# P transposes and row sums behind the eighth K tile, a last weight load in two single-row pieces, and a result signalled per column tile

## The chip, the cores and the metric

The kernel runs on one core of one Trainium2 chip. Times are device microseconds (us) of one execution. The kernel before takes 193.18 us, the median of four runs (193.08 to 195.44).

## What is computed

One decode step (one token, batch 8, width 512) of a block made of sliding-window attention over a cache, then a small multi-layer perceptron. Inputs are bfloat16. Cut to what matters:

```python
# attention: 32 query heads, 8 key/value heads, head size 128, window of the last 2048 of 8192 positions
q = layernorm(x) @ wq
scores = einsum("bhqd,bhkd->bhqk", q, k_window) * 128 ** -0.5
h = x + einsum("bhqk,bhkd->bhqd", softmax(scores), v_window) @ wo
# MLP: for one token the token-shift branch is zero, so x1 = xb
xb = layernorm(h)
out = h + xb + gelu(layernorm(xb) @ w3) @ w4      # w3: 512 x 1792, w4: 1792 x 512
```

For each of the 8 batches the windows of K and of V are 4 MB each. With `wq`, `wo`, `w3` and `w4` the core reads 79 MB from HBM.

## The kernel before, in words

**Loads.** SyncE (SP) issues nearly all loads on one queue, in a fixed list: `wq`, then K of batch 0 (two halves of four KV heads, 2 MB each), the first V half of the last batch, a first part of `wo`; then, for b = 0 to 6, the two K halves of batch b+1 and the two V halves of batch b; then the other V half of the last batch, the rest of `wo`, `w3`, `w4`. Every half has one buffer ("slot"), so SP waits before it reloads it: for a K half until TensorE has read the previous contents (`sem_Thi`, L239 to L240), for a V half until the PV product has read them (`sem_PV`, L241 to L242). `w4` (L260 to L267) goes into slot 0 once the last batch's first K half has been read, in pieces of 8, 4 and 2 blocks of 128 rows; within a piece, four (or, in the last, two) consecutive rows of `w4` lie together in a partition, and `w3_col` picks the matching columns of `w3`.

**A block.** TensorE works through 8 blocks, block i for batch i (`pe_block`, L561). The steps are:

- T(t), t = 0 to 7 (`pe_T`): 16 transposes of a K tile into one of two PSUM buffers `kT_ps`. ScalarE copies the low half out (`act_Elo`), VectorE the high half (`dve_Ehi`). A T that reuses a buffer waits for both copies of the tile two before.
- QK(t) (`pe_QK`): 4 matmuls of the copied tile with the queries, which collect the scores of all eight tiles in one bank of `S_ps`.
- `dve_max` (row maximum, five instructions), then `act_exp` twice (the exponentials into `P_sb`, the row sums into `lsum`).
- P(0), P(1) (`pe_P`): 8 transposes each of the previous batch's `P_sb`, into the same two `kT_ps` buffers; `dve_pT` masks them into `pT_sb`.
- LB (`pe_LB`): the row sums of the previous batch; `dve_rL` takes their reciprocal.
- PV (`pe_PV`): 128 matmuls of the previous batch's `pT_sb` with V; `dve_O1` scales, `pe_OP` reorders, `act_OP` stores into `opl`.

All orders are written by hand: TensorE's in `pe_block`, ScalarE's and VectorE's in the lists `AC` and `DV` (L602 to L619). In the kernel before, TensorE's block is: T0 to T3; P0, P1, LB of the previous batch; QK0, QK1; T4, QK2, T5, QK3, T6, QK4, T7, QK5; QK6, QK7; PV and OP of the previous batch. VectorE does `dve_pT` twice and `dve_rL` between its fourth and fifth copy. T4 and T5 take over the buffers of P0 and P1 and so wait for `dve_pT`.

**The end.** `pe_last` does P, LB, PV and OP of the last batch; then come the `wo` projection, the two layer norms, `w3`, gelu, and `pe_fin`: 14 blocks of `w4`, four matmuls each, one for each quarter of the 512 columns ("column tile" j, at partitions 32j). `pe_fin` waits for each piece of `w4` and signals after its last matmul. VectorE (`dve_final`) copies quarters 0 and 1, ScalarE (`act_final`) quarters 2 and 3, and SP stores the result.

Of the kernel before, what the change touches and what calls it, by code (L numbers as in the profile page):

```python
# [21 lines left out]
FC = F // 128  # L22
# [6 lines left out]
NT = 4  # L29
# [7 lines left out]
def bass_sequential_preLN__sliding_block_cached__mixer_s_mlp__decode_kernel(  # L37
# [24 lines left out]
    with es:  # L62
        sb = lambda shape, dtype, name: es.enter_context(nc.sbuf_tensor(name, shape, dtype))
        ps_t = lambda shape, dtype, name: es.enter_context(nc.psum_tensor(name, shape, dtype))
        S = lambda name: es.enter_context(nc.semaphore(name))
# [61 lines left out]
        NQ = 4  # L127
# [15 lines left out]
        sem_x = S("sem_x")  # L143
        sem_wq = S("sem_wq")
        sem_w3 = [S(f"sem_w3_{i}") for i in range(2)]
        sem_w4 = [S(f"sem_w4_{i}") for i in range(3)]
        sem_wo = [S(f"sem_wo{i}") for i in range(3)]
        sem_out = S("sem_out")

# [67 lines left out]

        NJ = DH // 4
        WO_CUT = [0, 8, 24, 32]
        W4_CUT = [0, 8, 12, 14]  # L220

        order = [("k", 0), ("k", 1), ("vl", 0), ("wo", 0)]
        for b in range(NB - 1):
# [191 lines left out]
        def need(e, sem, n):  # L415
            d = n - taken.setdefault(sem, 0)
            if d > 0:
                taken[sem] = n
                log.append((sem, d))
                if e is not None:  # L420
                    e.wait_ge(sem, d).then_inc(sem, -d)  # L421

        def pe_T(e, i, t):
            p = 2 * NT * i + t
            gq = t // NT
            if t % NT == 0:
                need(e, sem_k[gq], 16 * (i + 1))
            if t in (4, 5):
                need(e, sem_pT, 2 * i + t - 3)
            elif t in (2, 3, 6, 7):  # L430
                need(e, sem_Elo, p - 1)
                need(e, sem_Ehi, p - 1)
            if e is None:
                return
            k0 = t % NT * CT * DH
            src = slots[:, gq, k0:k0 + CT * DH]
            for c in range(CT):
                ins = e.matmul(kT_ps[t % 2][:, c * 128:(c + 1) * 128], src[:, c * 128:(c + 1) * 128],  # L438
                               perm_b[:, :], is_transpose=True)
                if c == CT // 2 - 1:  # L440
                    ins.then_inc(sem_Tlo, 1)
                if c == CT - 1:
                    ins.then_inc(sem_Thi, 1)

        def pe_P(e, i, half):
            need(e, sem_exp, 2 * i + half + 1)
            n = min(2 * NT * i + 3 + half, 2 * NT * NB)
            need(e, sem_Elo, n)
            need(e, sem_Ehi, n)
            if e is None:  # L450
                return
            for c in range(CT // 2):
                k = half * CT // 2 + c
                ins = e.matmul(kT_ps[half][:, c * 128:(c + 1) * 128], P_sb[:, k * 128:(k + 1) * 128],  # L454
                               perm_p[:, :], is_transpose=True)
            ins.then_inc(sem_PT, 1)
# [9 lines left out]
        def pe_QK(e, i):  # L466
            b, t = divmod(i, 2 * NT)
            gq, qi = divmod(t, NT)
            need(e, sem_Elo, i + 1)
            need(e, sem_Ehi, i + 1)  # L470
            if t == 0:
                need(e, sem_qc, b + 1)
            if e is None:
                return
            kv = kT_sb[:, i % NKT, :].rearrange("d (c g p) -> d g c p", p=PP, g=GL)
            o = 32 - R - R * t
            for gl in range(GL):
                ins = e.matmul(S_ps[32 * gl:32 * (gl + 1), 0, :], qcur[:, GL * gq + gl, o:o + 32],  # L478
                               kv[:, gl, :, :], start=(t == 0), stop=(t == 2 * NT - 1),
                               tile_position=(0, 32 * gl), skip_group_check=True)  # L480
            ins.then_inc(sem_QK, 1)
# [25 lines left out]
        def pe_LB(e):  # L507
            if e is not None:
                for half in range(2):
                    ins = e.matmul(LB, lspread[:, :, :].rearrange("p q h -> p (q h)"), lsum[:, half:half + 1],  # L510
                                   start=(half == 0), stop=(half == 1))
                ins.then_inc(sem_LB, 1)
# [6 lines left out]
        def dve_pT(e, b, half):  # L519
            e.wait_ge(sem_PT, 2 * b + half + 3)  # L520
            if b < 0 and half == 0:
                e.wait_ge(sem_pool, POOL_PT)
            m = mask16[:, :, :]
            h0 = half * CT // 2
            e.tensor_tensor(bass.AP(tensor=pT_sb[:, :, :, :].tensor, offset=h0 * NT * 48,  # L525
                                    ap=[[CT * NT * 48, 128], [48, CT // 2 * NT], [32, 2], [1, 16]]),
                            kT_ps[half][:, 0:W // 2].rearrange("p (c a x) -> p c a x", a=2, x=16),
                            bass.AP(tensor=m.tensor, offset=m.offset, ap=[m.ap[0], [0, CT // 2 * NT], [0, 2], [1, 16]]),
                            ALU.mult).then_inc(sem_pT, 1)
# [30 lines left out]

        def pe_block(e, i, later=None):  # L561
            p = 2 * NT * i
            for t in range(NT):
                pe_T(e, i, t)
            pe_P(e, i, 0)
            pe_P(e, i, 1)
            pe_LB(e)
            pe_QK(e, p)
            pe_QK(e, p + 1)
            for t in range(NT, 2 * NT):  # L570
                pe_T(e, i, t)
                pe_QK(e, p + t - 2)
            pe_QK(e, p + 6)
            pe_QK(e, p + 7)
            if i == 0:
                return
            with nullcontext() if e is None else e.If_ne(later, 0):
                log.append("later")
                for gq in range(2):
                    need(e, sem_v[gq], 16 * i)  # L580
                    if e is not None:
                        pe_PV(e, 2 + gq, gq)
                pe_OP(e, i - 1)
# [18 lines left out]
        for i in range(NB):  # L602
            p = 2 * NT * i
            for t in range(2 * NT):
                AC.append(lambda e, n=p + t: act_Elo(e, n))
                DV.append(lambda e, n=p + t: dve_Ehi(e, n))
                if t == 3:
                    DV.append(lambda e, i=i: dve_pT(e, i - 1, 0))
                    DV.append(lambda e, i=i: dve_pT(e, i - 1, 1))
                    if i:  # L610
                        DV.append(lambda e, i=i: dve_rL(e, i - 1))
            AC.append(lambda e, i=i: act_exp(e, i, 0))
            AC.append(lambda e, i=i: act_exp(e, i, 1))
            DV.append(lambda e, i=i: dve_max(e, i))
            if i + 1 < NB:
                DV.append(lambda e, i=i: dve_qc(e, i + 1))
            if i:
                DV.append(lambda e, i=i: dve_O1(e, i - 1))
                AC.append(lambda e, i=i: act_OP(e, i - 1))  # L619
# [99 lines left out]
        PEP_H3 = ev_pe.next()  # L719

        def w3_col(kc, fc):
            j = 4 if fc < W4_CUT[2] else W4_CUT[3] - W4_CUT[2]
            c0 = fc // 4 * 4
            return w3_sb[:, kc, c0 * 128:(c0 + j) * 128].rearrange("r (p j) -> r j p", j=j)[:, fc - c0, :]

        def pe_h3(e):
# [17 lines left out]
            e.activation(gT[:, :], misc[:, H3], ACT.Gelu_apprx_tanh).then_inc(sem_actP, 1)  # L744
        AC.append(act_gelu)

        PEP_FIN = ev_pe.next()

        def pe_fin(e):
            e.wait_ge(sem_dveP, DVEP_RES)  # L750
            for half in (hpx_hi, hpx_lo):
                for k in range(KC):
                    e.matmul(fin_ps[32 * k:32 * k + B, :], half[:, k * B:(k + 1) * B], ident_b[:, :],
                             start=(half is hpx_hi), stop=False, tile_position=(0, 32 * k), skip_group_check=True)
            e.wait_ge(sem_actP, ACTP_G)
            ins = None
            for fc in range(FC):
                if fc in W4_CUT:
                    e.wait_ge(sem_w4[W4_CUT.index(fc)], 16)
                for j in range(NQ):  # L760
                    ins = e.matmul(fin_ps[32 * j:32 * j + B, :], gT[:, fc * B:(fc + 1) * B],  # L761
                                   w4_sb[:, fc, j * DQ:(j + 1) * DQ], start=False, stop=(fc == FC - 1),
                                   tile_position=(0, 32 * j), skip_group_check=True)
            ins.then_inc(sem_peP, 1)
        PE.append(pe_fin)

        DVEP_OUT_READY = ev_dve.next()

        def dve_final(e):
            e.wait_ge(sem_peP, PEP_FIN)  # L770
            for j in range(NQ // 2):
                ins = e.tensor_copy(out_sb[:, j * DQ:(j + 1) * DQ], fin_ps[32 * j:32 * j + B, :])  # L772
            ins.then_inc(sem_dveP, 1)
        DV.append(dve_final)
# [1 line left out]
        ACTP_OUT_READY = ev_act.next()  # L776

        def act_final(e):
            e.wait_ge(sem_peP, PEP_FIN)
            for j in range(NQ // 2, NQ):  # L780
                ins = e.activation(out_sb[:, j * DQ:(j + 1) * DQ], fin_ps[32 * j:32 * j + B, :], ACT.Copy)
            ins.then_inc(sem_actP, 1)
        AC.append(act_final)
# [47 lines left out]
```

## Time and profile before

| quantity | value |
|---|---|
| median of four runs | 193.18 us (193.08 to 195.44) |
| the profiled execution, own time | 194.05 us |
| its span, first to last instruction | 192.3 us |
| mean granted TensorE clock | 0.913 |
| TensorE busy (matmuls) | 145.4 us, 76% |
| ScalarE busy | 93.4 us, 49% |
| VectorE busy | 85.9 us, 45% |
| the load queue, share of 16 DMA engines | 97.2% |
| read from HBM | 79.18 MB, 412 GB/s over the span |

Busy times say how much of the span an engine had an instruction in work; a load is split over 16 DMA engines, and the queue's share is the time of its packets over all sixteen. The rows of SP tell when a load was issued; the trace also holds, for each load, the moment at which each of the 16 engines marked its share as done. All positions below are us from the start of the span.

### The profile page before, as it was taken

What the parts mean: (1) busy time and instruction counts of PE and PEld (TensorE: products, weight loads), DVE (VectorE), ACT (ScalarE), POOL (GpSimd) and SP (SyncE); (2) the same over time, 40 slices, a digit from 0 to 9 for tenths busy, and PEclk for the clock granted to TensorE, in tenths of its full rate; (3) what the DMA queues carried; (4) which work ended last, traced back from release to release, by engine and by line L of the source; (5) the groups of instructions that cost most, each with busy time, mean ns of one, the idle gap of its engine ahead of it and who ended that gap; (6) DMA issues with size and microseconds to landing.
All of it is one profiled execution on the core that took longest, in us unless ns stands there. A gap on an engine that the chain in (4) does not pass through costs nothing. (4 is left out here: it accounts for less than half of the span.)

```text
span 192.3 us, 6348 instructions
## 1 busy us (share of the span) xinstructions
PE 145.4 (76%) x2848; PEld 118.3 (62%) x2848; DVE 85.9 (45%) x183; ACT 93.4 (49%) x119; POOL 6.4 (3%) x17
## 2 busy tenths in 40 slices
PE   2038997499759985996499979995999499785754
PEld 0014964487658765774497669674967487574642
DVE  7922655164606461745045535551455164530031
ACT  3031745666456446664254658445744585443041
POOL 8400000000000000000000000000000000000000
PEclk9999999799987999999759987999699999999655
DMA  6999999999999999999999999999999999999990
GB/s 220 436 436 433 423 412 440 372 426 429 433 435 429 436 433 438 419 426 433 426 433 433 436 429 436 436 429 426 426 433 426 433 433 436 429 436 409 409 400 34
DMA packets 6329, 79.31 MB, mean 412 GB/s; under 512 B 672, under 2 KB 688, under 8 KB 1712
## 3 DMA queue, kind: packets, MB, share of 16 engines
q1 hardware_dynamic: 6304, 79.18, 97.2%
q8 instruction: 6, 0.10, 0.2%
q14 instruction: 3, 0.02, 0.0%
q10 hardware_dynamic: 16, 0.01, 0.0%
HBM read 79.18 MB, written 0.01 MB: 412 GB/s over the span
## 5 line engine op out<-in xcount | busy, mean ns | idle before, releaser
L460 ACT ACTIVATE kT_sb<-kT_ps 128x1024 bf16<-128x1024 bf16 x64 | 64.9, 1024 | 49.7 <-PE kT_ps L438 49.6
L438 PE MATMUL kT_ps<-perm_b,slots 128*128 128x128 bf16 x1024 | 75.5, 239 | 13.8 <-PEq L421 13.8
L438 PEld LDWEIGHTS kT_ps<-perm_b,slots 128*128 128x128 bf16 x1024 | 68.3, 108 | 24.0 <-issue 23.7
L464 DVE COPY kT_sb<-kT_ps 128x1024 bf16<-128x1024 bf16 x64 | 44.3, 692 | 67.3 <-PE kT_ps L438 67.3
L503 ACT ACTIVATE P_sb<-S_ps,mtile 128x1024 bf16<-128x1024 f32 x16 | 17.7, 1110 | 19.4 <-DVE mtile L498 19.4
L478 PE MATMUL S_ps<-kT_sb,qcur 128*32 128x512 bf16 x256 | 22.6, 387 | 2.9 <-PEq L421 2.9
L535 PE MATMUL misc<-slots,pT_sb 128*32 128x128 bf16 x1024 | 16.4, 219 | 1.9 <-PEq L421 1.8
L535 PEld LDWEIGHTS misc<-slots,pT_sb 128*32 128x32 bf16 x1024 | 14.8, 97 | 3.5 <-issue 3.3
L525 DVE TENSOR_TENSOR pT_sb<-kT_ps,mask 128x1024 bf16<-128x1024 bf16 x18 | 12.3, 688 | 3.5 <-PE kT_ps L454 3.5
L454 PE MATMUL kT_ps<-perm_p,P_sb 128*128 128x128 bf16 x144 | 10.8, 218 | 3.0 <-PEq L421 3.0
L478 PEld LDWEIGHTS S_ps<-kT_sb,qcur 128*32 128x32 bf16 x256 | 5.5, 93 | 10.1 <-issue 6.6
L454 PEld LDWEIGHTS kT_ps<-perm_p,P_sb 128*128 128x128 bf16 x144 | 8.4, 97 | 4.8 <-issue 4.4
L554 PE MATMUL b<-o_sum,selw 128*128 128x32 f32 x56 | 7.3, 275 | 4.3 <-PEq L421 4.3
L554 PEld LDWEIGHTS b<-o_sum,selw 128*128 128x128 f32 x56 | 6.8, 191 | 5.3 <-issue 5.3
L487 DVE TENSOR_REDUCE mtile<-S_ps 128x1 f32<-128x512 f32 x8 | 5.5, 692 | 5.0 <-PE S_ps L478 5.0
L286 DVE TENSOR_SCALAR ident_f<-iota_f 128x128 f32<-128x128 f32 x1 | 5.7, 5689 | 1.3 <-POOL iota_f L207 1.3
L344 PE MATMUL b<-ident_b,xln_b 8*128 8x8 bf16 x4 | 0.3, 175 | 7.5 <-DVE xln_b L320 7.5
L287 DVE TENSOR_SCALAR ident_b<-iota_f 128x128 bf16<-128x128 f32 x1 | 5.6, 5614 | 0.0
L668 PE MATMUL S_ps<-opl,slots 128*128 128x8 bf16 x128 | 3.8, 167 | 2.3 <-issue 1.5
L344 PEld LDWEIGHTS b<-ident_b,xln_b 8*128 8x128 bf16 x4 | 0.2, 116 | 8.4 <-DVE xln_b L320 8.4
L544 DVE TENSOR_SCALAR o_sum<-misc,rL 128x128 f32<-128x128 f32 x8 | 2.8, 351 | 5.7 <-PE misc L535 5.7
L668 PEld LDWEIGHTS S_ps<-opl,slots 128*128 128x128 bf16 x128 | 3.5, 100 | 2.5 <-issue 1.6
(91 smaller groups left out, 67.7 us busy)
## 6 DMA issues: line engine op xcount, KB each, us to landing
slots<-in_A_k_cache_dram SPq DMA_DIRECT2D x16, 2048.0 KB, 12.8
slots<-in_A_v_cache_dram SPq DMA_DIRECT2D x16, 2048.0 KB, 17.3
slots<-in_A_wq_dram SPq DMA_DIRECT2D x1, 4096.0 KB, 12.1
slots<-in_A_wo_dram SPq DMA_DIRECT2D x2, 1024.0 KB, 21.9
slots<-in_A_wo_dram SPq DMA_DIRECT2D x1, 2048.0 KB, 27.4
slots<-in_B_w_dram SPq DMA_DIRECT2D x2, 896.0 KB, 31.7
slots<-in_B_w_dram SPq DMA_DIRECT2D x1, 1024.0 KB, 30.4
slots<-in_B_w_dram SPq DMA_DIRECT2D x1, 512.0 KB, 28.9
```

Source lines behind the costliest of these rows:

```text
L286: e.tensor_single_scalar(ident_f[:], iota_f[:], 0.0, ALU.is_equal)
L287: ins = e.tensor_single_scalar(ident_b[:], iota_f[:], 0.0, ALU.is_equal)
L438: ins = e.matmul(kT_ps[t % 2][:, c * 128:(c + 1) * 128], src[:, c * 128:(c + 1) * 128], perm_b[:, :], is_transpose=True)
L454: ins = e.matmul(kT_ps[half][:, c * 128:(c + 1) * 128], P_sb[:, k * 128:(k + 1) * 128], perm_p[:, :], is_transpose=True)
L460: e.activation(kT_sb[:, i % NKT, 0:W // 2], kT_ps[i % 2][:, 0:W // 2], ACT.Copy).then_inc(sem_Elo, 1)
L464: e.tensor_copy(kT_sb[:, i % NKT, W // 2:W], kT_ps[i % 2][:, W // 2:W]).then_inc(sem_Ehi, 1)
L478: ins = e.matmul(S_ps[32 * gl:32 * (gl + 1), 0, :], qcur[:, GL * gq + gl, o:o + 32], kv[:, gl, :, :], start=(t == 0), stop=(t == 2 * NT - ...
L503: e.activation(P_sb[:, half * W // 2:(half + 1) * W // 2].rearrange("r (k g) -> r k g", g=GL), bass.AP(tensor=S_ps[:, :, :].tensor, offset ...
L525: e.tensor_tensor(bass.AP(tensor=pT_sb[:, :, :, :].tensor, offset=h0 * NT * 48, ap=[[CT * NT * 48, 128], [48, CT // 2 * NT], [32, 2], [1, ...
L535: ins = e.matmul(pv_ps[32 * q:32 * (q + 1), :], pT_sb[:, c, q, 16 * gq:16 * gq + 32], slots[:, slot, k * DH:(k + 1) * DH], start=(gq == 0 ...
L554: ins = e.matmul(op_ps(b), selw[:, q, :], o_sum[:, NJ * q:NJ * (q + 1)], start=(q == 0), stop=(q == 3))
L668: ins = e.matmul(hT_ps[:, k * B:(k + 1) * B], wo_at(h)[:, k * 128:(k + 1) * 128], opl[:, h, :], start=False, stop=(h == NJ - 1), skip_grou ...
```

## The change

Three parts. In `pe_block`, P0, LB and P1 of the previous batch move from behind T3 to behind T7 (P0 and LB ahead of QK6, P1 ahead of QK7), QK(t-2) now follows T(t) from t = 2 on, and a wait for both `dve_pT` stands ahead of PV; T4 and T5 wait for the copies of T2 and T3 as their neighbours do. VectorE's `dve_pT` and `dve_rL` move behind its eighth copy. In `w4`, the last piece of two row blocks becomes two pieces of one, with 1 KB instead of 2 KB for each partition. At the end, the last matmul of each column tile signals by itself; VectorE copies tiles 0 and 2, ScalarE 1 and 3, each after its own signal.

```diff
-        sem_w4 = [S(f"sem_w4_{i}") for i in range(3)]
+        sem_w4 = [S(f"sem_w4_{i}") for i in range(4)]
-        W4_CUT = [0, 8, 12, 14]
+        W4_CUT = [0, 8, 12, 13, 14]
@@ pe_T
-            if t in (4, 5):
-                need(e, sem_pT, 2 * i + t - 3)
-            elif t in (2, 3, 6, 7):
+            if t > 1:
                 need(e, sem_Elo, p - 1)
                 need(e, sem_Ehi, p - 1)
@@ pe_P
-            n = min(2 * NT * i + 3 + half, 2 * NT * NB)
+            n = min(2 * NT * i + 7 + half, 2 * NT * NB)
@@ pe_block
-            for t in range(NT):
-                pe_T(e, i, t)
-            pe_P(e, i, 0)
-            pe_P(e, i, 1)
-            pe_LB(e)
-            pe_QK(e, p)
-            pe_QK(e, p + 1)
-            for t in range(NT, 2 * NT):
+            pe_T(e, i, 0)
+            pe_T(e, i, 1)
+            for t in range(2, 2 * NT):
                 pe_T(e, i, t)
                 pe_QK(e, p + t - 2)
+            pe_P(e, i, 0)
+            pe_LB(e)
             pe_QK(e, p + 6)
+            pe_P(e, i, 1)
             pe_QK(e, p + 7)
+            need(e, sem_pT, 2 * i + 2)
@@ the lists of ScalarE and VectorE, for each batch, after the eight copies
-                if t == 3:
-                    DV.append(lambda e, i=i: dve_pT(e, i - 1, 0))
-                    DV.append(lambda e, i=i: dve_pT(e, i - 1, 1))
-                    if i:
-                        DV.append(lambda e, i=i: dve_rL(e, i - 1))
+            DV.append(lambda e, i=i: dve_pT(e, i - 1, 0))
+            DV.append(lambda e, i=i: dve_pT(e, i - 1, 1))
+            if i:
+                DV.append(lambda e, i=i: dve_rL(e, i - 1))
@@ w3_col
-            j = 4 if fc < W4_CUT[2] else W4_CUT[3] - W4_CUT[2]
-            c0 = fc // 4 * 4
+            j = 4 if fc < W4_CUT[2] else 1
+            c0 = fc // j * j
@@ pe_fin
-            ins.then_inc(sem_peP, 1)
+                    if fc == FC - 1:
+                        ins.then_inc(sem_peP, 1)
@@ dve_final; act_final likewise with range(1, NQ, 2)
-            e.wait_ge(sem_peP, PEP_FIN)
-            for j in range(NQ // 2):
+            for j in range(0, NQ, 2):
+                e.wait_ge(sem_peP, PEP_FIN[j])
```

More of the change, by code (lines that the diff above doesn't have):

```diff
@@ L745, in bass_sequential_preLN__sliding_block_cached__mixer_s_mlp__decode_kernel @@
         AC.append(act_gelu)
-        PEP_FIN = ev_pe.next()
+        PEP_FIN = [ev_pe.next() for _ in range(NQ)]
         def pe_fin(e):
@@ L778, in act_final @@
         def act_final(e):
-            e.wait_ge(sem_peP, PEP_FIN)
-            for j in range(NQ // 2, NQ):
+            for j in range(1, NQ, 2):
+                e.wait_ge(sem_peP, PEP_FIN[j])
                 ins = e.activation(out_sb[:, j * DQ:(j + 1) * DQ], fin_ps[32 * j:32 * j + B, :], ACT.Copy)
```

## The prediction

> **What bounds the kernel now.** I read the page's slices and its chain first.
>
> ```profile
> PE   2038997499759985996499979995999499785754
> DMA  6999999999999999999999999999999999999990
> GB/s 220 436 436 433 423 412 440 372 426 429 433 435 429 436 433 438 419 426 433 426 433 433 436 429 436 436 429 426 426 433 426 433 433 436 429 436 409 409 400 34
> ...
> DMA 15%; PE 3%; SPq 1%; DVEq 0%; DVE 0%; issue 0%
> ```
>
> The DMA engines are busy in every slice but the first and last, at some 433 GB/s, and the chain that ended last is mostly a load. TensorE has gaps. So the load stream is the bound, and an edit counts only where it changes how the stream runs or what follows its end.
>
> The eighth slice (33.6 to 38.4 us) has only 372 GB/s. The windows view, cut to about the length of a 2 MB load, isolates it (last columns: TensorE clock, DMA share, GB/s):
>
> ```profile
> 29.20:34.00 4.80, 3.06 (x46) 1.86 (x43) 2.79 (x7) 2.11 (x3) 0.00 (x0) 1.00 1.04 440
> 34.00:38.80 4.80, 2.51 (x24) 2.54 (x25) 0.94 (x4) 3.32 (x5) 0.00 (x0) 0.68 0.99 369
> 38.80:43.60 4.80, 4.37 (x69) 3.95 (x68) 3.28 (x6) 3.07 (x3) 0.00 (x0) 0.96 1.02 437
> ```
>
> Busy, yet 15% slower: 16 KB packets that take 0.611 us elsewhere take up to 1.75 us just after 34.3. The timeline of 29 to 31.5 us shows the load that starts there, the second K half of batch 1:
>
> ```profile
> 30.24 1.07 PE L438 MATMUL kT_ps<-perm_b,slots 128*128 128x128 bf16 x16
> ...
> 31.34 0.54 SPq L246 DMA_DIRECT2D slots<-in_A_k_cache_dram  x1
> ```
>
> It is issued when T7 of block 0 ends. The first DMA engine finishes the load before it at 34.37: SP had a **lead** of 3.03 us over the engines. The smallest lead of any other K load is the one issued at 108.77, first needed at 112.70: 3.93 us, and its first engine finishes 4.84 us later, as undisturbed ones do. The load at 31.34 takes 5.25. I read this as a load issued almost too late.
>
> The stall has a second price. Before it, 14 of the 16 engines finish a load within 0.39 us of each other; after it they are spread over 1.68 us, and never close up. At 175.88 a packet of TensorE's instructions (the six of queue 8) holds up an engine that is then 0.91 to 0.94 us behind the first; it is 2.46 behind afterwards. A load counts as landed when its last engine is done, and this one is last to the end: the last piece of w4 is done on the first engine at 187.10, on the last at 189.42. The timeline of the end shows who waits:
>
> ```profile
> 188.85 0.31 PEld L761 LDWEIGHTS b<-slots,gT 128*8 128x8 bf16 x16 [0.40 <-DMA slots<-in_B_w_dram]
> 189.46 0.11 PEld L761 LDWEIGHTS b<-slots,gT 128*8 128x8 bf16 x8 [0.30 <-DMA slots<-in_B_w_dram]
> 189.90 0.57 DVE L772 CAST xln_b<-b 8x128 bf16<-8x128 f32 x2 [4.39 <-PE b L761]
> 189.90 0.56 ACT L781 ACTIVATE xln_b<-b 8x128 bf16<-8x128 f32 x2 [3.06 <-PE b L761]
> 190.55 0.37 SPq L270 DMA_DIRECT2D out_dram<-xln_b  x1
> ```
>
> **Part 1, the order of the block.** In block 0, T4 stands 2.42 us behind T3 (P0 starts at 23.83, T4 at 26.25): two P, LB, QK0, QK1. In the new order only QK0 and QK1 lie there, each adding 0.26 (the pitch of a T with its QK is 1.33 from 28.91 to 30.24, a T alone 1.07): T4 at about 24.4, T7's end and the issue at 29.5 instead of 31.34. The lead becomes 34.37 - 29.5 = 4.9 us, above the 3.93 that caused nothing. K's first half is issued one QK later (24.1 for 23.88), needed at 29.51: lead 5.4. The V halves stand behind in SP's list and are issued 1.8 us earlier too.
>
> In the other blocks, with the last one's rows: T0 at 153.16, T2 at 155.1, then six at 1.33, T7 ends at 162.8 (before: 164.57). Then P0 0.61, LB 0.4, QK6, P1 0.61, QK7 until 165.3, second dve_pT 165.1 to 165.8. PV starts at 166.0 (before 165.76), dve_max at 166.0, behind dve_rL (before 165.92). A block is 0.1 to 0.25 us longer on that path; what hides it is TensorE's idle wait for K, 1.8 us ahead of T0 at 153.16, and SP's lead. The second V half lands at 167.61 and holds the second half of PV anyway, so the end's chain does not see it. V's release waits behind dve_pT now, and who waits for it is SP with its V loads: their leads are 10 us and more. Without that cover it would cost 8 x 0.25 = 2 us.
>
> The gain, if the stall goes: the first engine is 0.39 earlier (5.25 - 4.86). The engine hit at 175.88 is 0.92 - 0.4 = 0.5 less behind. That would bring its end from 189.42 to 188.5. Next are engines that end at 188.9 (1.84 behind the first); they gain at least the 0.28 us by which the landing of the stalled load is late (5.14 after its predecessor against 4.86): 188.6. So w4 lands 0.8 us earlier. The wo pieces, landing on the same late engine at 178.35 and 180.79, move as well, so projection, norms and gelu follow: gelu's 186.84 becomes about 186, still ahead of the first piece of w4 (187.57, then 186.8). Ends: 0 (the stall has another cause), 0.28 (only the late landing), 1.2 (every engine gains 0.39 and the spread of 0.8 more). I take 0.8, since the packet rows point to the same engine from 175.88 to the end.
>
> The Trainium skill, "DMA: Bandwidth & Descriptors", section Specifications, speaks against this: it puts the first byte of a load issued by SyncE at about 0.6 us, so 3.03 us of lead would be ample and the earlier issue would bring nothing. By that rule the sum would be without the 0.8. I go by the row, because no other load with a larger lead stalls.
>
> **Part 2, w4 in single rows.** Each engine moves 16 packets of 1 KB instead of 8 of 2 KB. 2 KB takes 84 ns; 1 KB takes 44 (the load of x) to 92 ns (the store of the result): 16 x 44 - 8 x 84 = +0.03 us, at most 16 x 92 - 8 x 84 = +0.8. One more completion mark, 9 ns. I take +0.04: the load of x is a load like this. SP issues one more, behind the one at 168.39; even if it waits for queue space until the next landing at 172.48, that is 16 us early. Behind the last landing 4 matmuls are left instead of 8: the two groups of four start at 189.466 and 189.529, so -0.06. The strides of w3 columns change no count of instructions.
>
> **Part 3, signals per tile.** The four matmuls of a group start within 8 ns, so tile 0 is not ready noticeably before tile 3: gain 0.01 at most. Two extra waits, already satisfied, lie between copies that follow at 13 to 20 ns; the nearest price is the 30 ns between VectorE's self-waiting steps (70.87 + 0.21 to 71.11): +0.03.
>
> Sum: -0.8 + 0.04 - 0.06 + 0.03 = -0.8 us. On the profiled execution: 194.05 to 193.25 (span 192.3 to 191.5). The median stands 0.87 below that execution: 193.18 to **192.4**.
>
> **Rivals.**
> - *The stall stays, or was not due to the issue.* For it: 3 us is long against the 0.8 us from the store's issue at 190.55 to its first packets at 191.34. Then only parts 2 and 3 remain: 193.2.
> - *Half of it.* The stall goes, but the packet of instructions meets another engine that is late for its own reason (two are 1.68 and 1.79 us behind before the stall, from instruction packets at 21.42 and 30.0). Then the landing gains 0.28 only: 192.9.
> - *The block becomes the bound* (slower). Place: QK7, dve_max, exp and then ACT's first copy of the next block, now with P1 and dve_pT ahead. Price: with the lower clock (windows at 0.84 as in 95 to 115 us) T0 to T3 took 6.5 us instead of 4, so a block loses 2.5 us; it decides from the point where idle wait (1.8) plus lead (3.9) are used up, over 5.5 us. If each of 8 blocks then ran 0.25 to 0.5 over, the time is 195 to 197. Against it: every block but the first waits for K.
> - *1 KB rows at the store's price* (slower): +0.8 with no gain elsewhere is 194.0.
>
> **How the numbers follow.** Forecast 0.52 (191.9 to 192.8); half 0.16 (192.9); nothing 0.18 (193.2); 1 KB rows dear 0.08 (193.4 to 194.0); block 0.06 (195 to 197). The range 191.9 to 193.5 leaves out about 0.15. One per cent is 1.9 us, and that is about what a measurement of this kernel can tell from no change: faster by more 0.03 (all engines gain 1.2 and the tail shortens with them), within 0.90, slower 0.07.
>
> **What would show it.** Right: the second K load of batch 1 issued near 29.5 us; the eighth slice near 430 GB/s; the last two matmul groups near 188.6; second-half T's followed by one QK each at a pitch of 1.33. Wrong: that slice still at 370 with the earlier issue (then the lead was not the cause), a new slice below 410, TensorE's wait for K gone before T0, or a gap between the last two pieces of w4 well over 0.4 us.

## The result, and the profile after

| | before | after |
|---|---|---|
| median | 193.38 us (78 executions) | 193.14 us (52 executions) |
| lowest, highest | 192.97, 195.63 | 192.86, 193.96 |
| ratio | | 0.9974, 95% interval 0.9963 to 0.9984 |
| the traced execution, own time | 194.05 us | 193.98 us |
| its span | 192.3 us | 192.2 us |

The kernel became 0.26% faster, that is 0.5 us by the ratio (the medians alone differ by 0.24): of the forecast sign, and short of the forecast 0.8. That 193.14 lies inside the forecast range of 191.9 to 193.5 says little, because the range also holds the 193.2 of no change, and no execution reached the forecast 192.4. The median of four from which the forecast started, 193.18, was also 0.2 below that of 78. The ratios of this document leave out an execution more than 1.5% above the fastest of its kernel; that concerns one, the 196.51 us under "The smallest lead". The lowest times hardly differ. The difference lies in the upper ones: 33 of 78 executions of the kernel before took more than 193.6 us, and 3 of 52 of the changed one.

The slices of the page of the kernel after, with its chain:

```profile
PE   2038997499769986896599859985898499888654
PEclk9999999799987999999789987999999859999655
DMA  6999999999999999999999999999999999999990
GB/s 220 436 430 433 426 416 440 423 436 423 436 428 433 433 433 428 430 426 436 430 430 433 433 433 433 430 430 430 430 436 426 430 433 436 430 433 410 411 366 17
...
PE 5%; issue 1%; DVE 1%; ACT 0%; ACTq 0%
```

The dip of the eighth slice is gone, 423 GB/s for 372. But the chain that ended last is now one of TensorE, VectorE and ScalarE, and no load: something else took over in this execution. The windows view of it, same stretches as before (last columns: TensorE clock, DMA share, GB/s):

```profile
29.20:34.00 4.80, 3.00 (x42) 2.02 (x38) 3.34 (x8) 1.02 (x1) 0.00 (x0) 1.00 1.04 442
34.00:38.80 4.80, 2.58 (x25) 2.61 (x26) 0.88 (x3) 3.32 (x5) 0.00 (x0) 0.69 1.01 430
38.80:43.60 4.80, 4.80 (x74) 3.81 (x72) 2.50 (x5) 3.93 (x4) 0.00 (x0) 0.95 1.01 434
```

430 GB/s for 369. SP's rows of the same trace show why, in the terms of the prediction:

```profile
29.74 0.53 SPq L246 DMA_DIRECT2D slots<-in_A_k_cache_dram  x1
30.31 1.53 SPq L246 DMA_DIRECT2D slots<-in_A_v_cache_dram  x2
```

The second K half of batch 1 is issued at 29.74 (forecast 29.5, before 31.34), 4.64 us ahead of the first DMA engine's need at 34.38; that engine finishes it at 39.27, 4.89 us later, instead of 5.25. The last piece of w4 has landed at 188.68 (forecast 188.6, before 189.42). So far the steps held. The end of the timeline shows what did not follow:

```profile
187.79 0.26 ACT L740 ACTIVATE gT<-misc 128x112 bf16<-128x112 f32 x1 [0.83 <-PE misc L729]
188.10 1.38 PEld L757 LDWEIGHTS b<-slots,gT 128*8 128x8 bf16 x56 [0.32 <-ACT gT L740]
188.11 1.67 PE L757 MATMUL b<-slots,gT 128*8 128x128 bf16 x56
189.80 0.58 DVE L769 CAST xln_b<-b 8x128 bf16<-8x128 f32 x2 [3.08 <-PE b L757]
190.47 0.37 SPq L270 DMA_DIRECT2D out_dram<-xln_b  x1
```

All 56 matmuls run in one go behind gelu (188.05, before 186.84): none waits for w4 any more. Gelu is late because the last block was. Its clock tells: 0.62 on the mean of 151 to 160 us, against 1.00 before.

```profile
151.00:160.00 9.00, 7.21 (x73) 6.27 (x74) 2.35 (x4) 3.82 (x5) 0.00 (x0) 0.62 1.00 430
```

So the traced executions, 194.05 and 193.98, are long for two different reasons. That is what the experiments had to sort out.

### The profile page after: what moved, and what is told of

It is laid out like the page before. It is cut to its first block, busy times and chain, and to the rows that moved or that the text cites. A ratio compares the mean times of both kernels' runs of the same rounds, so it can differ in the third digit from the quotient of the medians.

```text
span 192.2 us, 6341 instructions
## 1 busy us (share of the span) xinstructions
PE 146.9 (76%) x2848; PEld 118.8 (62%) x2848; DVE 85.8 (45%) x183; ACT 94.3 (49%) x119; POOL 6.4 (3%) x17
## 5 line engine op out<-in xcount | busy, mean ns | idle before, releaser
L476 PE MATMUL S_ps<-kT_sb,qcur 128*32 128x512 bf16 x256 | 25.8, 393 | 0.0
L476 PEld LDWEIGHTS S_ps<-kT_sb,qcur 128*32 128x32 bf16 x256 | 6.6, 93 | 6.0 <-issue 0.2
L367 PE MATMUL S_ps<-slots,xlnT 128*8 128x512 bf16 x32 | 3.6, 628 | 1.9 <-DMA slots<-in_A_wq_dram 1.9
```

## The experiments

Four theories stand in the expectations. **L**: a load issued with too small a lead stalls, and the new order enlarges the lead. **E**: the gain comes from w4's single-row pieces and the signals. **T**: it comes from TensorE's order as such. **C**: the time is lost in the chain behind the last K load, when TensorE's clock is lowered there. "Lead" is always the time from SP's issue to the first DMA engine's end of the load ahead.

**Part 1 alone.** The changed kernel with w4, the signals and the copies as before.

```diff
-        W4_CUT = [0, 8, 12, 13, 14]
+        W4_CUT = [0, 8, 12, 14]
...
-        PEP_FIN = [ev_pe.next() for _ in range(NQ)]
+        PEP_FIN = ev_pe.next()
```

> Part 1 alone: the new order of the block, with w4 and the end as before. Theory L (the second K half of batch 1 was issued 3.03 us ahead of its need, too late; the new order issues it 1.6 us earlier): ratio to the kernel before 0.997, that load issued near 29.7 us, the window from 34.0 to 38.8 us at 430 GB/s, first DMA engine done with it at 39.25. Theory E (the gain is that of the single-row pieces and of the signals per tile): ratio 1.000. Theory T (the gain is TensorE's, from the blocks' order itself): ratio 0.997 as well, this run does not part it from L.

Ratio 0.9965 (0.9940 to 0.9991), 193.20 us; none of 12 executions above 193.6. The load was issued at 29.47, lead 4.77; first engine done at 39.14; w4 landed at 188.41, and the execution traced took 193.03 us. The gain is there without parts 2 and 3: it is in the order of the block, or what it does to SP.

**Parts 2 and 3 alone.** The kernel before with the rest of the diff.

```diff
-        W4_CUT = [0, 8, 12, 14]
+        W4_CUT = [0, 8, 12, 13, 14]
...
-        PEP_FIN = ev_pe.next()
+        PEP_FIN = [ev_pe.next() for _ in range(NQ)]
```

> Parts 2 and 3 alone: w4 in two single-row pieces and signals per column tile, with the old order of the block. Theory L: the stall at 34 us is there (about 370 GB/s from 34.0 to 38.8), ratio 1.000, at most 0.001 to either side. Theory E: ratio 0.997. Theory T: 1.000.

Ratio 1.0015 (0.9984 to 1.0045), which excludes a gain of 0.3%; E falls. 5 of 12 executions lie above 193.6, as in the kernel before. The stall, though, was missing from the trace (first line below), and that execution took 192.84 us. Its first K half was issued at 22.20 instead of 23.88, the second at 29.66, a lead of 4.57, with the old order. So the lead of the old order is not the same in each execution.

```profile
34.00:38.80 4.80, 2.30 (x22) 2.33 (x23) 0.40 (x1) 1.99 (x3) 0.00 (x0) 0.50 1.00 423
```

**More lead without touching TensorE.** The kernel before, a larger first piece of wo.

```diff
-        WO_CUT = [0, 8, 24, 32]
+        WO_CUT = [0, 16, 24, 32]
```

> The kernel before with one number changed: the first piece of wo has 16 rows for each partition instead of 8 (cuts 0, 16, 24, 32), so 1 MB more lies ahead of batch 1's K and the late load has a lead of 3.03 + 2.43 = 5.5 us with TensorE's order untouched. Theory L: the stall goes, ratio 0.997, as with the new order. Theories E and T: ratio 1.000.

A miss: ratio 1.0059 (1.0035 to 1.0082). The lead was 5.6 us and there was no stall, but all K and V came 2.43 us later, and the end could not take that: w4 landed at 188.59, gelu ended only at 189.96, and the result was stored at 192.37. The lowest time is 194.60. The median is 1.4 us above the kernel before, so by an estimate the chain behind the last K load has 2.43 - 1.4 = 1.0 us to spare in the kernel before (0.8 by the lowest times, 194.60 against 193.02). The edit was a bad test of L, and a rough measure of the cover at the end.

**Less lead in the changed kernel.**

```diff
-        WO_CUT = [0, 8, 24, 32]
+        WO_CUT = [0, 2, 24, 32]
```

> The changed kernel with one number changed: the first piece of wo has 2 rows for each partition instead of 8 (cuts 0, 2, 24, 32), so 0.75 MB less lies ahead of batch 1's K and the load's lead falls from 4.64 to 2.8 us, below the 3.03 of the kernel before. Theory L: the stall is back, between 34 and 38 us less its 1.8 us shift, and the ratio to the kernel before is 1.000 to 1.002. Theories E and T: no stall matters, ratio 0.997.

Half a miss: ratio 0.9979 (0.9951 to 1.0007), which doesn't part the theories. The lead was 3.12 and the stall was there, but small, 406 GB/s in 32.5 to 37.3 us and 0.24 us for the first engine; w4 still landed at 188.58, and only one of 12 executions lies above 193.6. So a lead of 3.1 us did not bring the long times back here, which speaks against L in its simplest form; the mean of the 16 engines lost 0.30 us in that load, and 0.74 in the kernel before.

**The smallest lead.** The same edit in the kernel before.

```diff
-        WO_CUT = [0, 8, 24, 32]
+        WO_CUT = [0, 2, 24, 32]
```

> The kernel before with the first piece of wo cut to 2 rows for each partition (cuts 0, 2, 24, 32), the old order of the block. All K and V loads come 1.8 us earlier, so the last block starts 1.8 us earlier, but the late load's lead falls from 3.03 to about 1.2 us. Theory L (the stall sets the time): a longer stall, 1 us or more at 32 us, ratio 1.003 to 1.008. Theory C (the kernel before loses time because the chain of the last block, with a lowered TensorE clock, ends after w4 has landed): that chain gets 1.8 us more room, ratio 0.996 to 0.998, and the longest times go.

Ratio 1.0012 (0.9988 to 1.0035): the nearer end of L's expectation, 1.003, lies inside the interval, and C's 0.998 or less outside. The times part into 7 of 193.02 to 193.35 and 5 of 194.03 to 196.51. The trace is of the longest. Two of its loads had leads of 1.18 and 1.97 us; the windows at their turn, and one undisturbed:

```profile
32.50:37.30 4.80, 3.11 (x36) 2.62 (x36) 2.25 (x7) 2.71 (x5) 0.00 (x0) 0.81 0.95 362
72.50:77.30 4.80, 3.11 (x122) 2.88 (x111) 1.58 (x7) 2.50 (x5) 0.00 (x0) 0.91 1.00 335
82.00:86.80 4.80, 4.40 (x67) 3.38 (x66) 2.75 (x5) 2.06 (x3) 0.00 (x0) 1.00 1.00 430
```

The second one lies in block 2: the stall is not a matter of block 0.

**A V half ahead of the late K half.** The kernel before with two entries of SP's list exchanged.

```diff
-            order += [("k", 2 * b + 2), ("k", 2 * b + 3), ("v", 2 * b), ("v", 2 * b + 1)]
+            four = [("k", 2 * b + 2), ("k", 2 * b + 3), ("v", 2 * b), ("v", 2 * b + 1)]
+            order += [four[j] for j in ((0, 2, 1, 3) if b == 0 else (0, 1, 2, 3))]
```

> The kernel before with two entries of SP's list exchanged for batch 0 only: the first V half ahead of the second K half of batch 1. Nothing changes for the last block, the sum of what lies ahead of each later load is the same; the late load now has 4.86 us more lead. Theory L: no stall at 34 us and ratio 0.997, as with the new order. Theory C: ratio 1.000.

A miss again: 1.0023 (0.9992 to 1.0054), 9 of 12 above 193.6. The stall at 34 us went (427 GB/s), as L says, and another came one batch later: K's second half of batch 1 now lands 4.86 us later, block 1 ends later, and the next one of its kind was issued at 51.48 with a lead of 2.31 us.

```profile
49.00:53.80 4.80, 4.44 (x136) 3.33 (x136) 2.83 (x6) 2.46 (x3) 0.00 (x0) 1.00 0.97 416
53.80:58.60 4.80, 4.11 (x109) 3.82 (x98) 2.18 (x7) 4.11 (x7) 0.00 (x0) 1.00 0.98 352
58.60:63.40 4.80, 4.49 (x71) 3.75 (x68) 2.96 (x6) 2.33 (x4) 0.00 (x0) 1.00 1.01 428
```

**The length of the last chain in the new order.** The changed kernel with cuts 0, 16, 24, 32.

```diff
-        WO_CUT = [0, 8, 24, 32]
+        WO_CUT = [0, 16, 24, 32]
```

> The changed kernel with the first piece of wo of 16 rows (cuts 0, 16, 24, 32), as e3_lead_up did to the kernel before (1.0059): every K and V load comes 2.43 us later, and the chain behind the last K load, no longer covered by w4, sets the end. So it measures the length of that chain in the new order against the old. My working of part 1: 0.1 to 0.25 us longer, ratio 1.0064 to 1.0072. A theory that the new order shortens the chain (P no longer holds up T4): 1.004 or less.

Ratio 1.0071 (1.0049 to 1.0093, 6 executions) against 1.0059 for the old order under the same edit. The difference, 0.0012 x 193.4 = 0.23 us, is what part 1's working gave for a block (0.1 to 0.25 us longer), but the intervals overlap; that the chain is much shorter in the new order is excluded.

**The kernel before, once more, twice.** No edit.

> The kernel before, unchanged, one more profiled execution. Theory L: the window from 34.0 to 38.8 us at 370 GB/s again, spread of the 16 engines' ends over 1 us. Theory C: a lowered clock during the last block (153 to 168 us), TensorE not waiting for the last piece of w4, if the execution is a long one.

> The kernel before, unchanged, a third profiled execution. Theory L: a lead of 3.0 us at the second K half of batch 1 goes with a stall and a time of 194 us; a lead of 3.3 us or more (when TensorE's clock rises earlier, as in the traced execution of e2_end) with no stall and 193.1 us.

The first took 194.14 us, the second 193.21. Windows of the first, then of the second:

```profile
19.00:22.00 3.00, 3.00 (x34) 3.00 (x33) 1.87 (x4) 1.78 (x2) 0.00 (x0) 1.00 0.99 421
...
34.00:38.80 4.80, 2.46 (x24) 2.49 (x25) 0.89 (x4) 3.32 (x5) 0.00 (x0) 0.64 0.96 365
```

```profile
19.00:22.00 3.00, 2.77 (x50) 2.60 (x47) 2.36 (x5) 2.76 (x4) 0.00 (x0) 1.00 1.01 431
...
34.00:38.80 4.80, 2.55 (x25) 2.58 (x26) 0.65 (x1) 1.98 (x3) 0.00 (x0) 0.50 1.01 427
```

The same program: 34 matmuls done in 19 to 22 us with a stall later, 50 without. In the second, TensorE's first transposes ran faster, and SP's rows answer:

```profile
22.18 8.00 SPq L246 DMA_DIRECT2D slots<-in_A_k_cache_dram  x2
30.23 1.25 SPq L246 DMA_DIRECT2D slots<-in_A_v_cache_dram  x2
```

The second of the two K issues in the first row is at 29.65, a lead of 4.72; in the first execution it is at 31.34, a lead of 3.02. The last piece of w4 lands at 188.57 and 189.51, and in both executions the chain that ended last runs through the load of w4; the line of the page is the same in both:

```profile
DMA 15%; PE 3%; SPq 1%; DVEq 0%; DVE 0%; issue 0%
```

The clock was lowered in the last block of both (154.8 to 158.2 us, 152.5 to 155.9), so C does not explain why the first one is long.

Why the transposes ran at different speeds is in the trace, though not in the windows, which show a clock of 1.00 where nothing is recorded. The first entry of the clock, at full speed, stands at 21.66 us in the first execution and at 15.95 in the second. Before it a transpose starts every 107 ns, the same as in the later stretches that are recorded at half clock; behind it, every 56 ns. It stands at 22.10 us in the traced execution of 194.05, and at 16.07 in that of parts 2 and 3 alone, which had a lead of 4.57. So in these four traces of the old order the moment at which TensorE gets its full clock sets the lead, and with it whether the load stalls.

**Only SP's issue held back.** The changed kernel; SP waits for one more count ahead of every second K half, in all batches. First until QK6 of the block before, then until QK7.

```diff
                         e.wait_ge(sem_Thi, NT * (t - 1))
+                        if t % 2:
+                            e.wait_ge(sem_QK, 2 * NT * b - 1)
```

```diff
+                            e.wait_ge(sem_QK, 2 * NT * b)
```

> The changed kernel, only SP holds back every second K half until QK6 of the block before (it waits for that in addition), which puts its issue back to about 31.3 us in block 0, where the kernel before has it, and as much later in the other blocks. TensorE's, VectorE's and ScalarE's orders and the end stay as changed. Theory L: the lead is 3.0 us again, a stall of 0.3 to 0.5 us from 34 us on, the engines' ends spread over more than the two late ones, and the times go back to those of the kernel before, ratio 0.999 to 1.002, long ones of 194 to 195 us among them. Theory C and the theory that the order itself helps: 0.997, as the changed kernel.

> As e9_late_issue, but SP holds back every second K half until QK7 of the block before, about 0.9 us later still: in block 0 an issue near 32.2 us, a lead of 2.2 to 2.4 us. Theory L, with the leads measured so far (1.2 to 2.3 us: first engine 0.75 to 1.1 us late): a stall of 0.6 us or more at 34 us and a ratio of 1.002 to 1.008 to the kernel before, above e9_late_issue's 1.0008. A theory that e9's time came from the extra wait as such and not from the lead: the same as e9, 1.001.

Medians 193.87 and 194.45 us; ratios 1.0008 (0.9987 to 1.0029) and 1.0042 (1.0013 to 1.0071); 8 and 11 of 12 above 193.6. With TensorE's, VectorE's and ScalarE's orders and the end all as changed, the gain is lost when SP issues about as late as in the kernel before, and turns into a loss when it issues later still. T and E can't give that. In the trace of the first the clock rose early, at 16.4 us, the lead was 3.32 and the stall small (first engine 4.97 us); in that of the second the lead was 2.55, and the window reads 403:

```profile
34.00:38.80 4.80, 2.67 (x26) 2.70 (x27) 0.69 (x1) 3.15 (x5) 0.00 (x0) 0.57 1.01 403
```

The stall itself was smaller than expected in both. In the second the first engine took 4.91 us, with the spread grown to 1.96; on the mean of the 16 engines the load lost 0.41 us, in the first 0.23, and 0.74 in the kernel before. So these runs show that a late issue costs the time, and not that the stall of this one load is all of the price.

**The changed kernel once more.** No edit.

> The changed kernel, unchanged, one more profiled execution. Theory L: no load with a lead below 3.2 us, no stall, w4's last piece done at 188.3 to 188.9. If the clock is not lowered during the last block, TensorE waits for the last piece of w4 and the result's store is issued near 189.6, against 190.47 in the profile where the clock was lowered from 151.9 to 158.7 us and the chain behind the last K load set the end.

193.09 us. No lead below 4.45, w4's last piece at 188.47, the clock lowered only from 152.2 to 155.6 us in the last block, and TensorE waits for w4:

```profile
188.51 0.09 PEld L757 LDWEIGHTS b<-slots,gT 128*8 128x8 bf16 x4 [0.24 <-DMA slots<-in_B_w_dram]
188.82 0.58 DVE L769 CAST xln_b<-b 8x128 bf16<-8x128 f32 x2 [3.71 <-PE b L757]
188.85 0.55 ACT L778 ACTIVATE xln_b<-b 8x128 bf16<-8x128 f32 x2 [2.43 <-PE b L757]
189.50 0.37 SPq L270 DMA_DIRECT2D out_dram<-xln_b  x1
```

**All loads together.** The fourteen traces hold 406 K and V loads behind the first ones. Time from the first engine's end of one load to its end of the next, and the same between the means of all 16 engines' ends, by lead:

| lead, us | first engine's time, us | mean of 16 engines, us | where |
|---|---|---|---|
| 1.18, 1.97 | 5.87, 5.99 | 6.07, 6.22 | before, wo cut at 2 |
| 2.31 | 5.61 | 5.94 | V half ahead |
| 2.44 | 5.00 | 5.10 | before, wo cut at 2 |
| 2.55, 2.98 | 4.91, 4.92 | 5.27, 5.08 | held until QK7 |
| 3.02, 3.03 | 5.28, 5.25 | 5.60, 5.60 | before, two executions |
| 3.12 | 5.10 | 5.16 | after, wo cut at 2 |
| 3.25, 3.29, 3.32, 3.43 | 4.85, 4.86, 4.97, 4.99 | 4.87, 4.87, 5.09, 4.97 | several |
| 3.45 and more (393 loads) | 4.86 median, at most 5.01 | 4.86 median, at most 4.97 | all |

The first engine alone misses part of it: three loads with leads of 2.4 to 3.0 us look nearly undisturbed there. On the mean of the engines every load with a lead of 3.12 us or less is late, by 0.2 us or more, and none of the 393. How late it is doesn't follow from the lead alone: 0.22 us at a lead of 2.98, 0.74 at 3.02.

## Why the prediction was right, and where it was short

**What bounds the kernel: right.** The load stream set the end of the kernel before in all three traces, that of the changed kernel in its second look (193.09), and that of part 1 alone (193.03), but not of the execution that took 193.98.

**The stall and its cause: right as far as the runs reach.** The stall goes with the order (part 1 alone), and is absent from an execution of the old order in which the lead happens to be 4.7. The late issue costs the time: the gain is lost when only SP's issue is held back (0.9987 to 1.0029, against 0.9963 to 0.9984 for the changed kernel). A stall comes back there too, but a smaller one, so that the price runs through the stall is argued and not shown. The weighing against the Trainium skill's first byte of 0.6 us ("DMA: Bandwidth & Descriptors", Specifications) came out for the row: behind a queue full of other loads, leads of 3.12 us and less cost 0.2 to 1.4 us here on the mean of the engines, leads of 3.45 and more at most 0.11. The page speaks of a first byte, not of a load behind others.

**The terms of part 1** (two traces of the changed kernel, then part 1 alone). Issue 29.5 forecast, 29.74, 29.90 and 29.47 measured; lead 4.9, measured 4.64, 4.45 and 4.77; first engine 0.39 us earlier, measured 0.35 (39.62 to 39.27); w4 landed 188.6, measured 188.68, 188.47 and 188.41. How the last engine gains the rest was half right. The prediction laid the spread of the ends to the stall; but in the first trace of the changed kernel, without a stall, the ends of that load are spread over 1.66 us, against 1.68. What the stall adds lies between the first and the last: the mean of the 16 ends stands 0.73 us behind the first, against 0.47. The packet of instructions near 176 us then moved the last end back by 1.03 us in the kernel before (1.43 to 2.46), and by 0.3 and 0.5 in the changed one (1.68 to 1.98 in its second trace, 1.55 to 2.06 in its first). In the second trace of the kernel before the last end fell back at the stall itself instead, from 1.85 to 2.22. No experiment here sets which engine an instruction packet meets, so part of this gain may be luck. The block's extra 0.1 to 0.25 us: 0.23, not separated from zero. "What hides it is TensorE's idle wait": yes, but the cover is thinner than the prediction took it. The second V half was to hold PV anyway; with the clock lowered in the last block, PV started at 168.32 behind dve_pT, after that V half had landed, and the chain ended 1.1 us behind w4. That is the traced execution of 193.98. The wo cut at 16 puts the cover at 0.8 to 1.0 us.

**Parts 2 and 3: right in being nothing.** In single rows the two pieces take 0.66 to 0.67 us together on the first engine, against 0.64 to 0.65 for the piece of two: about +0.02 where +0.04 was taken, and far from the +0.8. From w4's landing to the store's issue it is 1.03 us in the changed kernel (188.47 to 189.50) and 1.13 in the kernel before (189.42 to 190.55, and 188.57 to 189.70): -0.10, where -0.03 was the sum. The interval of the run, 0.9984 to 1.0045, can't see that.

**The step that failed** is the last of the sum: "On the profiled execution: 194.05 to 193.25 (span 192.3 to 191.5). The median stands 0.87 below that execution: 193.18 to 192.4." The first sentence was borne out where the end isn't held up otherwise: 193.09 for the changed kernel in its second trace, 193.03 for part 1 alone. The second carried the gain over to a median that didn't pay the price. The 0.87 us between the traced execution and the median were the stall, or most of it: an execution of the kernel before with a lead of 4.72 took 193.21, and those with 3.02 and 3.03 took 194.14 and 194.05. Of 78 executions, 33 took over 193.6, on the mean 194.34, and the other 45 193.22, about what the changed kernel takes. So 33 stand to gain some 1.1 us and the others nothing: 0.42 x 1.1 = 0.5 us on the mean, as the ratio says, and 0.24 by the medians. That all 33 are long through a small lead, and a clock that rises late, is argued from three traces of this kernel, not shown. The prediction had the sign of it in hand, a traced execution 0.9 us above the median, and treated it as an offset.

**The rivals.** "The stall stays": its 193.2 is the number nearest to the measured median, but the stall went. "Half of it" gave 192.9, closer to the measured median than the forecast, but by a landing that gains only 0.28 us; it gained 0.74 and 0.95 in the traces of the changed kernel. "The block becomes the bound" did occur, once among the traces, at 193.98, not 195 to 197, and in the last block alone: in both traces of the changed kernel the clock is lowered in four stretches ahead of it, and the leads stay at 4.45 us and more. "1 KB rows at the store's price": no.

**What stays open.** Why some 3.2 us and not 1 is the lead that is needed. How the price comes about beyond the stall: in the trace of the kernel held until QK6 the stall was 0.11 us for the first engine, yet the last engine ended 3.0 us behind it. It fell from 1.6 to 2.3 us behind in the load that ended at 59 us, with a packet of instructions at 56.8, and from 2.2 to 3.2 near the one at 176.58. And why with a wo cut at 2 seven executions of the kernel before still took 193.0 to 193.4: an early clock is a guess, since the one trace is of a long execution, with its first clock entry at 21.81 us.

## What to carry to other kernels

Where a queue of loads is the bound, look for the load with the smallest time between its issue and its turn, and measure that against the loads that don't stall: an engine's order can matter only because it decides when a buffer is given back. Measure a stall on all the engines, not on the first alone. A gain read off one traced execution belongs to executions like it; before it is taken off the median, ask whether the median pays that price, and a traced time well above the median is the first sign that it doesn't. A step that hides behind idle time at full clock must be costed once more at the lowered clock, in the last stage above all, where nothing comes after it.

## What the runs showed of the hardware that was not expected

Every load issued 3.12 us or less before its turn took 0.2 to 1.4 us longer on the mean of the sixteen DMA engines (nine loads; 393 with 3.45 us or more, at most 0.11), although the engines had work until then. The engines don't close up again after a disturbance: from 60 to 172 us the spread of their ends stays within 0.2 us in thirteen of the fourteen traces, at some value between 1.4 and 2.5 us. Around a packet of instructions near 176 us the last end fell further behind the first by 1.0 to 1.6 us in three traces (2.19 to 3.16, 1.59 to 3.14 and 1.43 to 2.46 us). And TensorE's first transposes start every 107 ns until the trace's first clock entry, and every 56 ns behind it; that entry stood at 22.1, 21.7 and 16.0 us in three executions of one program, and in these it went with whether a load stalled 10 us later.
